# Moving everything after attention off GpSimd, one-instruction gate, and two parts of a product kept in TensorE's queue

## The chip, the core and the metric

The kernel runs on one core of a Trainium2 chip. A core has five engines that each work through their own instructions in order: TensorE (PE in the rows; its weight loads are PEld), VectorE (DVE), ScalarE (ACT), GpSimd (POOL) and SyncE (SP), which here issues nearly all DMAs. They wait for each other by semaphores. The metric is the time of one execution on the device, in microseconds (us).

## The reference

Rotary attention, then a mixture layer with a squared ReLU, then a second layer with a sigmoid gate. Only the two layers matter here, on 2304 tokens of 512 features, with 2048 features inside:

```python
h = x @ w_in;  r = np.maximum(h, 0.0);  x = (s * (r * r) + b) @ w_out       # first layer
h = x @ w_in2; g = h * (1.0 / (1.0 + np.exp(-1.702 * h)));  out = g @ w_out2  # second layer
```

Results are fp32, inputs of the products are split into a high and a low part, and three products of parts stand for one fp32 product.

## The kernel before

**Stages.** Attention runs first, with the first layer's early passes of 256 tokens woven in. When attention is over (`widen`, some 685 us into the run) its buffers are closed and `late` is set. Then come the end of the first layer (what is left of a pass of 256 tokens, pass 8, and pass 9 with 512) and, beside it, the preparation of the second layer's weights; then the second layer: passes 10 to 13 with 512 tokens and pass 14 with 256.

**Order.** TensorE's instructions are chained in the order in which the code is written (`mm` pins each to the one before); from `late` on VectorE's are too (`dv`). ScalarE's and GpSimd's are placed by a list scheduler. SyncE issues its DMAs in the scheduler's order, and each DMA that must wait holds all behind it.

**End of the first layer** (`first_layer`, L965). For each of 16 blocks of the inner features, TensorE makes 12 matmuls into a bank `l`, then 12 matmuls of the second product of the block two steps back (`SKEW = 2`). Between the two, each 256 columns pass ScalarE's Relu (L980), GpSimd's square (L990) and `s*r+b` (L991), ScalarE's copy to the high part (L992) and VectorE's low part (L993).

**Weights of the second layer.** Raw weights come by DMA into three buffers, `raw`; a buffer is filled again when its job is done (`fill`, `take`, `done_with`). `outer_make` (L820) takes two for each of 8 groups, turns fp64 words into fp32 (`to_f32`: L570 on ScalarE, L573, L578, L584 on VectorE), forms four differences on GpSimd (L844), and splits seven matrices into high (ScalarE, L834) and low (VectorE, L841). `combine` (L760) takes one raw per group: four sums on GpSimd (L790), highs L780, lows L787. `convert(budget)` draws such steps between blocks. The weights' scale and each pass's scale travel through DRAM (`share_top`: a DMA `tops<-xm`, then a broadcast DMA `xc<-tops`).

**Second layer** (`seven`, L1119). Each pass has 8 groups of 256 inner features. Both products of a group are done as seven half-size products (Strassen-Winograd). The first product's seven go alternately into two banks (`a0` and `b0`, tiles `l`): VectorE adds them into `cb` and `ca` (`add`, L1144; `u` is the first of them). The gate is ScalarE's Tanh into a tile `r` (L1148) and VectorE's `(r+1)*c` (L1152). Then come a difference on VectorE (L1190), three sums on GpSimd (`mixed`, L1155), and highs (ScalarE, L1158) and lows (VectorE, L1161) of seven operands: two in `gs`, four in `gb`, one in a spare weight slot `wo`. `rest`, `rest2` and `rest3` hold the last of it; `side(0)` to `side(2)` of the next group run them. The second product's first six parts (`products`) go to a `queue`; `between()` issues one at three places inside the next group's seven, and then the queue is emptied:

```python
                mixed = seven(n, g, x, between, side, need)
                yield
                tail.extend(mixed[3:6])
                while queue:
                    between()
                queue += second(n, g, mixed)
```

**Next tokens.** While a pass runs, `side` also loads and prepares the next pass's tokens (`sums_work`): maxima, scale, four differences (`sums_less`, on GpSimd, L1086), and seven splits (`x_high` L1067, `x_low` L1072).

Of the kernel before, what the change touches and what calls it, by code (L numbers as in the profile page):

```python
# [9 lines left out]
F32 = mybir.dt.float32  # L10
# [4 lines left out]
AF = mybir.ActivationFunctionType  # L15
# [8 lines left out]
X_TOP = 2.0**12  # L24
X_MIN = 2.0**-50
H_SCALE = 2.0**-23


@with_exitstack
def kernel(  # L30
# [729 lines left out]
    def combine(g, tag):  # L760
        pool = wpool if tag else late["m2"]
        raw = take()
        if tag == "stage":
            wc = [
                late["m2"].tile([128, k, 2, 256], F16, tag=tag, name=f"wc{g}{k}", bufs=3) for k in (4, 3)
            ]
            wc = [t[:, j] for t, k in zip(wc, (4, 3)) for j in range(k)]
        else:
            wc = pool.tile([128, 7, 2, 256], F16, tag=tag or f"wc{g}", name=f"wc{g}", bufs=1)
            wc = [wc[:, j] for j in range(7)]  # L770
        tmp = moe.tile([128, 2, 256], F32, tag="gg", name=f"sum{g}", bufs=3)
# [12 lines left out]

        def later():
            lo, src, col, hi = pend.pop(0)
            dv(nc.vector.scalar_tensor_tensor(lo, src, col, hi, op0=ALU.mult, op1=ALU.subtract))  # L787

        def mixed(o, x, y, op):
            nc.gpsimd.tensor_tensor(o, x, y, op=op)  # L790

        mixed(sa, a[:, 1, 0], a[:, 1, 1], ALU.add)
        halves(0, a[:, 0, 0], up)
        yield 0.1
        mixed(sb, sa, a[:, 0, 0], ALU.subtract)
# [24 lines left out]
    def outer_make(g, tag):  # L820
        up = wscale[:, 4:5]
        parts = [
            late["m2"].tile([128, k, 2, 256], F16, tag="g", name=f"wm{g}{k}", bufs=3) for k in (4, 3)
        ]
        tmp = moe.tile([128, 2, 256], F32, tag="gg", name=f"wsum{g}", bufs=3)

        pend = []

        def halves(j, src, n=1):
            o = parts[j // 4][:, j % 4 : j % 4 + n]  # L830
            hi, lo = o[:, :, 0], o[:, :, 1]
            if n == 1:
                hi, lo = hi[:, 0], lo[:, 0]
            pace(nc.scalar.activation(hi, src, AF.Copy, scale=up))  # L834
            pend.append((lo, src, hi))
            if len(pend) > 1:
                later()

        def later():
            lo, src, hi = pend.pop(0)  # L840
            dv(nc.vector.scalar_tensor_tensor(lo, src, up, hi, op0=ALU.mult, op1=ALU.subtract))  # L841

        def less(o, a, b):
            nc.gpsimd.tensor_tensor(o, a, b, op=ALU.subtract)  # L844
# [24 lines left out]
        done_with(1)  # L869
        nc.sync.dma_start(made[g][1], parts[1])  # L870
# [25 lines left out]
    late = {}  # L896
# [68 lines left out]
    def first_layer(n, f, w, xh, xl):  # L965
# [11 lines left out]
        for i in range(T // TB):  # L977
# [3 lines left out]
            if not late:  # L981
# [5 lines left out]
                    gl[:, cols], r, sb[:, 1:2], f32(gh[:, cols]), op0=ALU.add, op1=ALU.subtract  # L987
                )
                continue
            nc.gpsimd.tensor_tensor(r, r, r, op=ALU.mult)  # L990
            nc.gpsimd.tensor_scalar(r, r, sb[:, 0:1], sb[:, 1:2], op0=ALU.mult, op1=ALU.add)  # L991
            nc.scalar.copy(gh[:, cols], r)  # L992
            dv(nc.vector.tensor_tensor(gl[:, cols], r, f32(gh[:, cols]), op=ALU.subtract))  # L993
        return gh, gl
# [3 lines left out]
    def sums_load(n):  # L998
# [4 lines left out]
        x["m"] = late["m2"].tile([128, 9], F32, tag="xm", name=f"xm{n}", bufs=3)  # L1003
# [25 lines left out]
    def sums_scale(x):  # L1029
        m = x["m"]  # L1030
        scales(m[:, 5:6], m[:, 6:7], x["row"])
        for o, a, col, factor in ((7, 6, 2, 0.851), (8, 7, 5, 0.5 / 0.851)):
            if o == 7:
                factor = factor / H_SCALE
            dv(
                nc.vector.tensor_scalar(
                    m[:, o : o + 1], m[:, a : a + 1], wscale[:, col : col + 1], factor, op0=ALU.mult, op1=ALU.mult
                )
            )

# [40 lines left out]
                x_low(x, *x_high(x, j))  # L1081
                del x["todo"][j]

    def sums_less(x):
        for o, a, b in sums_parts(x):
            nc.gpsimd.tensor_tensor(o, a, b, op=ALU.subtract)  # L1086

    def sums_work(x):
        sums_top(x, 0, 0)
        yield  # L1090
        sums_top(x, 0, 1)
        sums_top(x, 1, 0)
        yield
        sums_top(x, 1, 1)
        yield
        yield
        sums_scale(x)
        pairs = [x_high(x, j) for j in (0, 3)]
# [20 lines left out]
    def seven(n, g, x, between, side, need):  # L1119
        T = PASSES[n][2]  # L1120
        half = T // 2
        nm = f"{n}_{g}"
        wc, xc, gain = combos[g], x["xc"], x["m"][:, 7:8]
        a0, b0 = (bank[:, 0:half] for bank in l1_banks[0:2])
        a1, b1 = a0, b0

# [16 lines left out]
        def add(o, ps, rest):  # L1143
            dv(nc.vector.scalar_tensor_tensor(o, ps, H_SCALE, rest, op0=ALU.mult, op1=ALU.add))  # L1144

        def curve(c, z):
            r = moe.tile([128, T], F32, tag="gg", name=f"r{nm}{z}", bufs=3)
            nc.scalar.activation(r, c, AF.Tanh, scale=gain)  # L1148
            return r

        def gate(c, r):
            dv(nc.vector.scalar_tensor_tensor(c, r, 1.0, c, op0=ALU.add, op1=ALU.mult))  # L1152

        def mixed(o, a, b, op):
# [40 lines left out]
        mixed(s3, a22, s3, ALU.subtract)
        mixed(a11, a11, s3, ALU.add)
        low(gb[:, 3, 1], a22, gb[:, 3, 0])
        high(gb[:, 0:2, 0], two(cb))

        def rest():  # L1200
            high(spare[:, 0, 0:half], a12)
            low(spare[:, 1, 0:half], a12, spare[:, 0, 0:half])
            mixed(a12, a12, s3, ALU.subtract)
            high(gb[:, 2, 0], a12)

        def rest2():
            low(gb[:, 0:2, 1], two(cb), gb[:, 0:2, 0])
# [19 lines left out]
    def products(n, g, made_g):  # L1227
# [105 lines left out]
    def experts():  # L1333
# [134 lines left out]
        for n in range(LAST0 + 1, len(PASSES)):  # L1468
            x = ahead.pop(n)
            for g in range(NG):  # L1470
                need(g, combos)

                def side(i):
                    if tail:
                        tail.pop(0)()
                    if n + 1 < len(PASSES):
                        x2nd = ahead.setdefault(n + 1, {})
                        if (g, i) == (0, 1):
                            x2nd.update(sums_load(n + 1))
# [12 lines left out]
                queue += second(n, g, mixed)  # L1492
                yield
# [264 lines left out]
```

## Time and profile before

| what | us |
|---|---|
| median of 3 runs (lowest, highest) | 1236.63 (1235.91, 1239.54) |
| the profiled execution itself | 1236.13 |
| its span, first to last instruction | 1234.3 |
| busy: PE, DVE, ACT, POOL | 1079.2, 959.7, 725.8, 478.6 |
| 0 to 686: attention and what is woven in | 686 |
| 686 to 868: end of the first layer, weights | 182 |
| 868 to 1234.3: second layer | 366.3 |

The profiled execution's own time is its span and 1.8 us around it. Times inside the profile count from the span's start. A matmul that follows others starts some 0.11 us after the one before but is listed with its whole duration, so a busy TensorE is not one at its peak.

### The profile page before, as it was taken

Reading aid. Unit: us, or ns where it says so; the run is one execution under the profiler, and the core shown is the slowest. Engines: PE = TensorE matmul, PEld = TensorE weight load, DVE = VectorE, ACT = ScalarE, POOL = GpSimd, SP = SyncE. Lnnn points to the kernel's source line nnn. Section 1 sums busy time; section 2 is a strip of 40 time slices with the busy share of each in tenths; the row PEclk is TensorE's granted clock in tenths of the full one; section 3 lists DMA queues with packets and bytes.
Section 4 is the critical chain, followed back from the end, with each engine's and each line's share of the span. In section 5 each row is a group of like instructions: output and inputs, shape, how many; then the busy total and the mean of one; then the engine's idle time right before and its main releaser. Section 6 shows DMA issues by size and latency. Waiting matters only on the chain.

```text
span 1234.3 us, 24890 instructions
## 1 busy us (share of the span) xinstructions
PE 1079.2 (87%) x8888; PEld 962.4 (78%) x8888; DVE 959.7 (78%) x2114; ACT 725.8 (59%) x1587; POOL 478.6 (39%) x557
## 2 busy tenths in 40 slices
PE   3676767898999999999999898878899898999997
PEld 2555557797888999999999786656788787888886
DVE  4877768999877887777776588756978887788876
ACT  2877766786665656576664564546554464554554
POOL 3344524344334332421111587866432424223222
PEclk9887988999999999999999899989999999999999
DMA  5776878899888889877776678754102001001010
GB/s 146 226 231 199 263 209 285 273 340 301 248 254 264 276 259 283 253 238 234 236 202 134 207 259 307 269 130 162 65 3 56 16 23 48 3 19 36 3 36 18
DMA packets 152778, 216.42 MB, mean 175 GB/s; under 512 B 34384, under 2 KB 107472, under 8 KB 152656
## 3 DMA queue, kind: packets, MB, share of 16 engines
q1 hardware_dynamic: 151792, 214.26, 55.9%
q8 instruction: 70, 1.15, 0.4%
q10 hardware_dynamic: 864, 0.59, 0.2%
q14 instruction: 52, 0.43, 0.1%
HBM read 157.65 MB, written 50.07 MB: 168 GB/s over the span
## 4 chain that ended last, share of the span: by engine, by line
PE 41%; DVE 23%; DMA 17%; ACT 7%; issue 5%; POOL 5%; SPq 2%; DVEq 0%; ACTq 0%; POOLq 0%
PE l L100 17%; PE acc L100 13%; PE t L100 3%; PE s L100 3%; DMA top<-in_moe_w_in_dram 3%; PE av L100 3%; DMA qb<-qsp 2%; DMA raw<-in_moe_w_out_dram 2%; DVE pt L499 2%; DVE P L432 2%; DMA w2f<-top 2%; DMA raw<-w2f 2%; POOL r L991 1%; DVE c L1152 1%; DVE wm L841 1%
## 5 line engine op out<-in xcount | busy, mean ns | idle before, releaser
L476 POOL TENSOR_SCALAR P<-P,st 128x576 f32<-128x576 f32 x108 | 85.0, 787 | 319.1 <-DVE st L475 185.8
L100 PE MATMUL l<-xc,wc 128*128 128x256 f16 (+1 forms) x1680 | 196.7, 264 | 10.5 <-DVE u L1144 6.7
L100 PEld LDWEIGHTS <-wc 128*128 128x128 f16 x1680 | 153.5, 98 | 32.4 <-issue 15.3
L100 PE MATMUL acc<-g,w 128*128 128x256 f32 (+1 forms) x1056 | 165.1, 304 | 14.5 <-DVE g L993 9.2
L100 PEld LDWEIGHTS acc<-g,w 128*128 128x128 f32 x1056 | 142.8, 194 | 25.7 <-DVE g L993 13.7
L442 ACT ACTIVATE P<-P,st 128x576 f32<-128x576 f32 x144 | 111.6, 775 | 65.3 <-DVE P L432 57.0
L1155 POOL TENSOR_TENSOR c<-c,c 128x256 f32<-128x256 f32 (+1 forms) x80 | 57.7, 721 | 236.3 <-DVE gs L1161 208.6
L432 DVE TENSOR_SCALAR_CACHE_REDUCE P<-s 128x576 f32<-128x576 f32 x144 | 108.0, 750 | 46.4 <-PE s L100 45.2
L100 PE MATMUL t<-ident,P 128*128 128x128 f32 x720 | 109.6, 286 | 29.1 <-DVE pt L499 18.7
L100 PE MATMUL l<-xh,w 128*128 128x256 f32 x616 | 126.7, 289 | 5.6 <-DVE r L982 2.9
L100 PEld LDWEIGHTS t<-ident,P 128*128 128x128 f32 x720 | 85.0, 147 | 38.4 <-issue 26.1
L100 PEld LDWEIGHTS l<-xh,w 128*128 128x128 f32 x616 | 101.9, 192 | 7.7 <-DVE r L982 3.7
L499 DVE TENSOR_TENSOR pt<-t,pt 128x640 f16<-128x640 f32 x108 | 88.3, 818 | 17.3 <-ACT pt L498 15.9
L1148 ACT ACTIVATE r<-c,xm 128x512 f32<-128x512 f32 (+1 forms) x80 | 54.3, 679 | 79.9 <-DVE c L1144 78.6
L100 PEld LDWEIGHTS <-gb 128*128 128x128 f16 x864 | 83.8, 98 | 10.5 <-ACT gb L1158 0.7
L100 PE MATMUL l<-xl,w 128*128 128x256 f32 x308 | 87.6, 284 | 1.2 <-DVE xl L948 1.2
L100 PE MATMUL s<-k,qb 128*128 128x320 f32 x480 | 87.0, 308 | 1.9 <-DVE pt L503 1.8
L100 PE MATMUL acc<-g,ws 128*128 128x256 f32 (+1 forms) x480 | 77.4, 309 | 11.0 <-ACT g L992 8.5
L275 POOL TENSOR_TENSOR rot<-nat,tab 128x288 f32<-128x288 f32 x60 | 52.9, 903 | 80.0 <-DMA nat<-in_k_dram 34.7
L498 ACT CAST pt<-t 128x640 f16<-128x640 f32 x108 | 73.8, 684 | 12.7 <-PE t L100 11.8
L100 PEld LDWEIGHTS s<-k,qb 128*128 128x128 f32 x480 | 72.4, 192 | 8.4 <-issue 3.1
L100 PEld LDWEIGHTS acc<-g,ws 128*128 128x128 f32 x480 | 65.3, 194 | 17.0 <-ACT g L992 9.8
(179 smaller groups left out, 2598.9 us busy)
## 6 DMA issues: line engine op xcount, KB each, us to landing
ws<-wd SPq DMA_DIRECT2D x80, 512.0 KB, 5.8
k<-ksp SPq DMA_DIRECT2D x24, 576.0 KB, 6.3
stage<-in_moe_w_in_dram SPq DMA_DIRECT2D x16, 512.0 KB, 5.5
stage<-in_moe_w_out_dram SPq DMA_DIRECT2D x16, 512.0 KB, 6.4
top<-in_moe_w_in_dram SPq DMA_DIRECT2D x32, 256.0 KB, 3.3
wo<-in_moe_w_out_dram SPq DMA_DIRECT2D x32, 256.0 KB, 5.6
raw<-in_moe_w_out_dram SPq DMA_DIRECT2D x16, 512.0 KB, 4.9
wd<-w SPq DMA_DIRECT2D x10, 512.0 KB, 4.0
```

The lines of the kernel that those rows point to most:

```text
L100: pin(nc.tensor.matmul(*args, **kw))
L275: eng.tensor_tensor(rot[:, :, e], st["nat"][:, :, 1 - e], tab[:, 2 - e], op=ALU.mult),
L432: ins = nc.vector.tensor_scalar(pr, ps[:, 192 : 192 + S], -Q_SCALE, None, op0=ALU.mult, op1=ALU.min, accum_out=st[:, 0:1],)
L442: nc.scalar.activation(pr, pr, AF.Exp, bias=st[:, 0:1], scale=-1.0, accum_out=total)
L476: pin(nc.gpsimd.tensor_scalar(pr, pr, st[:, 2:3], 1.0, op0=ALU.mult, op1=ALU.mult), "pool")
L498: nc.scalar.copy(hi, pc)
L499: nc.vector.tensor_tensor(lo, pc, hi, op=ALU.subtract)
L841: dv(nc.vector.scalar_tensor_tensor(lo, src, up, hi, op0=ALU.mult, op1=ALU.subtract))
L991: nc.gpsimd.tensor_scalar(r, r, sb[:, 0:1], sb[:, 1:2], op0=ALU.mult, op1=ALU.add)
L1148: nc.scalar.activation(r, c, AF.Tanh, scale=gain)
L1152: dv(nc.vector.scalar_tensor_tensor(c, r, 1.0, c, op0=ALU.add, op1=ALU.mult))
L1155: nc.gpsimd.tensor_tensor(o, a, b, op=op)
```

## The change

GpSimd's work from `late` on goes to other engines: squares and `s*r+b` to ScalarE (Square, Identity), the sums of `combine`, `outer_make`, `seven` and the next tokens to VectorE. The gate becomes one ScalarE instruction, Silu, in place; the scale that Tanh's form carried is now applied with the high and low parts (`lift`). The four differences of the next tokens are drawn one by one, and the first operands of a group are split per half. Two parts of the second product stay in the queue at the end of each group. Cut to its core:

```diff
@@ combine, outer_make, seven: mixed and less
-            nc.gpsimd.tensor_tensor(o, x, y, op=op)
+            dv(nc.vector.tensor_tensor(o, x, y, op=op))
@@ first_layer
-            nc.gpsimd.tensor_tensor(r, r, r, op=ALU.mult)
-            nc.gpsimd.tensor_scalar(r, r, sb[:, 0:1], sb[:, 1:2], op0=ALU.mult, op1=ALU.add)
+            nc.scalar.activation(r, r, AF.Square)
+            nc.scalar.activation(r, r, AF.Identity, bias=sb[:, 1:2], scale=sb[:, 0:1])
@@ sums_work
         sums_top(x, 1, 1)
-        yield
+        for o, a, b in sums_parts(x):
+            yield
+            mixed_x(o, a, b)
@@ seven
-        def curve(c, z):
-            r = moe.tile([128, T], F32, tag="gg", name=f"r{nm}{z}", bufs=3)
-            nc.scalar.activation(r, c, AF.Tanh, scale=gain)
-            return r
-        def gate(c, r):
-            dv(nc.vector.scalar_tensor_tensor(c, r, 1.0, c, op0=ALU.add, op1=ALU.mult))
+        def curve(c):
+            nc.scalar.activation(c, c, AF.Silu, scale=gain)
-            nc.scalar.copy(hi, c)
+            nc.scalar.activation(hi, c, AF.Copy, scale=lift)
-            dv(nc.vector.tensor_tensor(lo, c, hi, op=ALU.subtract))
+            dv(nc.vector.scalar_tensor_tensor(lo, c, lift, hi, op0=ALU.mult, op1=ALU.subtract))
@@ seven, behind the last product
-        rb, ra = curve(cb, 1), curve(ca, 0)
-        gate(cb, rb)
...
-        dv(nc.vector.tensor_tensor(s3, a11, s3, op=ALU.subtract))
-        high(gs[:, :, 0], two(cb))
-        gate(ca, ra)
-        low(gs[:, :, 1], two(cb), gs[:, :, 0])
+        curve(cb)
+        curve(ca)
+        s3 = p1
+        high(gs[:, 0, 0], a11)
+        mixed(s3, a11, a21, ALU.subtract)
+        low(gs[:, 0, 1], a11, gs[:, 0, 0])
+        high(gs[:, 1, 0], s3)
         high(gb[:, 3, 0], a22)
-        mixed(s3, a22, s3, ALU.subtract)
-        mixed(a11, a11, s3, ALU.add)
+        side(3)
+        mixed(a21, a21, a22, ALU.add)
+        low(gs[:, 1, 1], s3, gs[:, 1, 0])
+        mixed(a11, a21, a11, ALU.subtract)
         low(gb[:, 3, 1], a22, gb[:, 3, 0])
         high(gb[:, 0:2, 0], two(cb))
@@ experts
-                        if (g, i) == (3, 1):
-                            sums_less(x2nd)
-                        if i in (2, 3) and (g in (1, 2) or g > 3):
+                        if g and (i > 1 or i and g > 5):
                             next(x2nd["work"], None)
-                while queue:
+                while len(queue) > 2:
                     between()
```

**GpSimd's rows in the first layer's last pass, before.** `r_80` and `r_81` are the two halves of block 8, `sum_10403` and `sum_10672` temporaries of two `combine` jobs, `raw_10400` the raw weights of the second of them.

```order
L990 TENSOR_TENSOR r_80_10437<-r_80_10437 128x256
L790 TENSOR_TENSOR sum_10403<-raw_10274 128x256
L990 TENSOR_TENSOR r_81_10443<-r_81_10443 128x256
L790 TENSOR_TENSOR sum_10672<-raw_10400 128x256
L991 TENSOR_SCALAR r_80_10437<-r_80_10437,sb 128x256
L790 TENSOR_TENSOR sum_10403<-raw_10274,sum_10403 128x256
L991 TENSOR_SCALAR r_81_10443<-r_81_10443,sb 128x256
```

The change has no such rows on GpSimd. The same first sum of `raw_10400` stands on VectorE there, behind the low parts of block 12 (`g_12`) and the last splits of pass 10's tokens (`xc`):

```order
L994 TENSOR_TENSOR g_12_10644<-r_120_10645,g_12_10644 128x256
L994 TENSOR_TENSOR g_12_10644<-r_121_10651,g_12_10644 128x256
L1077 SCALAR_TENSOR_TENSOR xc_10147<-xt_1_10514,xm_10146,xc_10147 128x512
L1077 SCALAR_TENSOR_TENSOR xc_10147<-xr_1_10145,xm_10146,xc_10147 128x512
L791 TENSOR_TENSOR sum_10674<-raw_10400 128x256
L791 TENSOR_TENSOR sum_10674<-sum_10674,raw_10400 128x256
```

The sum that needs `raw_10400` moved from the middle of block 8 to behind block 12.

**TensorE's rows at the change of a group, before.** In the second layer's pass 10, `l_1774` and `l_9163` are the banks `a0` and `b0`, `wc_10341` and `wc_10402` the first product's weights of groups 2 and 3, `gs_2` and `gb_1` operands of the second product of groups 2 and 1, `acc` and `l_9165` its banks. Six matmuls with their weight loads make one part; one row of each part is shown.

```order
L100 MATMUL acc_3_10955<-wo_10150,gb_1_10961 128x256
...
L100 MATMUL l_9164<-wo_10150,gb_1_10961 128x256
...
L100 MATMUL l_9165<-wo_10150,gb_1_10961 128x256
...
L100 MATMUL l_1774<-xc_10147,wc_10402 128x256
...
L100 MATMUL l_9163<-xc_10147,wc_10402 128x256
...
L100 MATMUL acc_0_10952<-wo_10266,gs_2_11077 128x256
```

The same place in the change:

```order
L101 MATMUL acc_1_10939<-wo_10150,gs_1_10946 128x256
...
L101 MATMUL acc_2_10940<-wo_10150,gb_1_10947 128x256
...
L101 MATMUL acc_3_10941<-wo_10150,gb_1_10947 128x256
...
L101 MATMUL l_1774<-xc_10147,wc_10402 128x256
...
L101 MATMUL l_9163<-xc_10147,wc_10402 128x256
...
L101 MATMUL l_9164<-wo_10150,gb_1_10947 128x256
...
L101 MATMUL l_9165<-wo_10150,gb_1_10947 128x256
...
L101 MATMUL acc_0_10938<-wo_10266,gs_2_11062 128x256
```

Where three of the old group's parts stood last and the new group's first part of the second product came after two products, now two old parts stand among the new products, and the part that reads `gs` of the group before comes behind six of the seven.

**VectorE's rows at the end of a group, before** (group 5 of pass 11, which prepares pass 12's tokens; `c_51` and `c_50` are `cb` and `ca`):

```order
L1144 SCALAR_TENSOR_TENSOR c_50_12436<-l_1774,u_5_12438 128x256
L1152 SCALAR_TENSOR_TENSOR c_51_12435<-r_51_12516,c_51_12435 128x512
L1190 TENSOR_TENSOR c_51_12435<-c_51_12435 128x256
L1152 SCALAR_TENSOR_TENSOR c_50_12436<-r_50_12518,c_50_12436 128x512
L1161 TENSOR_TENSOR gs_5_12439<-c_51_12435,gs_5_12439 128x2x256
L1161 TENSOR_TENSOR gb_5_12440<-c_50_12436,gb_5_12440 128x256
L1072 SCALAR_TENSOR_TENSOR xc_11830<-xr_1_11828,xm_11829,xc_11830 128x512
L1144 SCALAR_TENSOR_TENSOR u_6_12553<-l_9163,p_6_12552 128x256
L1161 TENSOR_TENSOR wo_10767<-c_50_12436,wo_10767 128x256
```

And in the change, from the same add on:

```order
L1152 SCALAR_TENSOR_TENSOR c_50_12390<-l_1774,u_5_12392 128x256
L1158 TENSOR_TENSOR p_5_12391<-c_51_12389 128x256
L1164 SCALAR_TENSOR_TENSOR gs_5_12393<-c_51_12389,xm_10865,gs_5_12393 128x256
L1077 SCALAR_TENSOR_TENSOR xc_11803<-xr_0_11800,xm_11802,xc_11803 128x512
L1158 TENSOR_TENSOR c_51_12389<-c_51_12389,c_50_12390 128x256
L1164 SCALAR_TENSOR_TENSOR gs_5_12393<-p_5_12391,xm_10865,gs_5_12393 128x256
L1158 TENSOR_TENSOR c_51_12389<-c_51_12389 128x256
L1164 SCALAR_TENSOR_TENSOR gb_5_12394<-c_50_12390,xm_10865,gb_5_12394 128x256
L1152 SCALAR_TENSOR_TENSOR u_6_12515<-l_9163,p_6_12514 128x256
L1164 SCALAR_TENSOR_TENSOR gb_5_12394<-c_51_12389,xm_10865,gb_5_12394 128x2x256
```

The two gate rows (L1152 before) and the wide low part are gone, three sums have come from GpSimd, and the token split (`xc`) that stood directly ahead of the next group's `u` now stands ahead of the sums.

## Rows read from the trace of the kernel before

**Rows 1.** The page's parts 1 and 4: busy engines; the chain that ended last.

```profile
PE 1079.2 (87%) x8888; PEld 962.4 (78%) x8888; DVE 959.7 (78%) x2114; ACT 725.8 (59%) x1587; POOL 478.6 (39%) x557
...
PE 41%; DVE 23%; DMA 17%; ACT 7%; issue 5%; POOL 5%; SPq 2%; DVEq 0%; ACTq 0%; POOLq 0%
```

**Rows 2.** Windows: length, PE, PEld, DVE, ACT, POOL busy, granted clock, DMA share, GB/s.

```profile
686.00:868.00 182.00, 154.27 (x829) 127.75 (x828) 136.93 (x227) 99.27 (x228) 135.40 (x160) 0.95 0.67 224
868.00:1234.30 366.30, 340.78 (x3164) 296.17 (x3162) 296.13 (x632) 186.78 (x404) 110.70 (x138) 0.99 0.11 27
820.40:827.20 6.80, 4.20 (x9) 3.02 (x10) 1.88 (x4) 2.55 (x7) 5.54 (x10) 0.50 0.23 78
948.00:1028.00 80.00, 74.85 (x674) 65.42 (x672) 66.17 (x131) 40.42 (x82) 24.93 (x28) 1.00 0.11 28
1045.60:1052.50 6.90, 5.78 (x29) 3.94 (x28) 3.90 (x8) 1.41 (x3) 2.64 (x4) 0.51 0.00 0
```

**Rows 3.** TensorE's waits, 868 to 1234.3: total us, times, longest.

```profile
PE acc L100 <- DVE gs L1161: 8.7, 19, 2.4
PE l L100 <- DVE u L1144: 6.7, 14, 1.7
PE acc L100 <- ACT gs L1158: 3.5, 7, 1.4
```

**Rows 4.** Timeline around 962: start, duration, engine, line; [idle before].

```profile
960.41 1.07 DVE L1152 SCALAR_TENSOR_TENSOR c<-r,c 128x512 f32<-128x512 f32 x1
...
960.88 1.71 POOL L1086 TENSOR_TENSOR xt<-xr,xt 128x512 f32<-128x512 f32 x1
...
962.80 1.75 DVE L1152 SCALAR_TENSOR_TENSOR c<-r,c 128x512 f32<-128x512 f32 x1
...
963.64 0.28 PE L100 MATMUL acc<-wo,gs 128*128 128x256 f16 x1 [1.41 <-ACT gs L1158]
...
965.21 0.72 PE L100 MATMUL acc<-wo,gs 128*128 128x256 f16 x5 [1.29 <-DVE gs L1161]
```

**Rows 5.** Timeline around 913: VectorE and TensorE.

```profile
912.67 1.22 DVE L1072 SCALAR_TENSOR_TENSOR xc<-xr,xm,xc 128x512 f16<-128x512 f32 x1
...
914.28 0.81 PE L100 MATMUL l<-xc,wc 128*128 128x256 f16 x6 [0.42 <-DVE u L1144]
```

**Rows 6.** Costs by line, 868 to 1234.3: count | busy us, mean ns.

```profile
L1152 DVE SCALAR_TENSOR_TENSOR c<-r,c 128x512 f32<-128x512 f32 x64 | 46.8, 730 | 0.2
L1148 ACT ACTIVATE r<-c,xm 128x512 f32<-128x512 f32 x63 | 45.4, 721 | 72.7 <-DVE c L1144 71.4 <-DVE gb L1161 1.3
...
L1161 DVE TENSOR_TENSOR gb<-c,gb 128x256 f16<-128x256 f32 x72 | 33.8, 469 | 1.6 <-ACT gb L1158 0.9
```

**Rows 7.** ScalarE's table load: ns of one, shortest, median, longest.

```profile
L309 ACT ACT_TABLE_LOAD  x1: 1283/1283/1283, 0.7 to 0.7; - x1
```

**Rows 8.** TensorE's waits, 686 to 868.

```profile
PE acc L100 <- ACT g L992: 12.7, 8, 5.8
PE acc L100 <- DVE g L993: 11.7, 12, 2.6
```

**Rows 9.** Timeline, 813 to 823.

```profile
813.55 8.41 SPq L745 DMA_DIRECT2D raw<-w2f  x2
...
819.61 0.72 POOL L790 TENSOR_TENSOR sum<-raw 128x256 f32<-128x256 f32 x1 [5.47 <-DMA raw<-w2f]
...
820.90 0.40 ACT L992 CAST g<-r 128x256 fp32r<-128x256 f32 x1 [6.97 <-POOL r L991]
...
822.59 0.79 PE L100 MATMUL acc<-g,ws 128*128 128x512 f32 x1 [5.78 <-ACT g L992]
```

**Rows 10.** Costs by line, 686 to 868.

```profile
L991 POOL TENSOR_SCALAR r<-r,sb 128x256 f32<-128x256 f32 x49 | 45.0, 921 | 1.9
...
L990 POOL TENSOR_TENSOR r<-r 128x256 f32<-128x256 f32 x49 | 37.3, 770 | 31.0 <-ACT r L980 30.6
...
L992 ACT CAST g<-r 128x256 fp32r<-128x256 f32 x49 | 19.2, 401 | 27.1 <-POOL r L991 26.5
```

More of the change, by code (lines that the diff above doesn't have):

```diff
@@ L26 @@
 H_SCALE = 2.0**-23
+G_TOP = 2.0**-22
 @with_exitstack
@@ L843, in less @@
         def less(o, a, b):
-            nc.gpsimd.tensor_tensor(o, a, b, op=ALU.subtract)
+            dv(nc.vector.tensor_tensor(o, a, b, op=ALU.subtract))
         one, _ = yield from to_f32(take())
@@ L1002, in sums_load @@
         x["raw"] = [f32(x_tile(f"xr{n}_{i}"))[:, 0 : 2 * T] for i in range(2)]
-        x["m"] = late["m2"].tile([128, 9], F32, tag="xm", name=f"xm{n}", bufs=3)
+        x["m"] = late["m2"].tile([128, 10], F32, tag="xm", name=f"xm{n}", bufs=3)
         finals[n] = x["m"][:, 8:9]
@@ L1031, in sums_scale @@
         scales(m[:, 5:6], m[:, 6:7], x["row"])
-        for o, a, col, factor in ((7, 6, 2, 0.851), (8, 7, 5, 0.5 / 0.851)):
-            if o == 7:
-                factor = factor / H_SCALE
+        for o, a, col, factor in (
+            (7, 6, 2, 1.702 / H_SCALE),
+            (9, 5, 0, G_TOP / 1.702),
+            (8, 6, 2, 1.0 / G_TOP),
+            (8, 8, 5, 1.0),
+        ):
+            b = m[:, a : a + 1]
             dv(
                 nc.vector.tensor_scalar(
-                    m[:, o : o + 1], m[:, a : a + 1], wscale[:, col : col + 1], factor, op0=ALU.mult, op1=ALU.mult
+                    m[:, o : o + 1], b, wscale[:, col : col + 1], factor, op0=ALU.mult, op1=ALU.mult
                 )
@@ L1082, in sums_split, with mixed_x @@
                 del x["todo"][j]
-    def sums_less(x):
-        for o, a, b in sums_parts(x):
-            nc.gpsimd.tensor_tensor(o, a, b, op=ALU.subtract)
+    def mixed_x(o, a, b):
+        dv(nc.vector.tensor_tensor(o, a, b, op=ALU.subtract))
     def sums_work(x):
@@ L1094, in sums_work @@
         sums_top(x, 1, 1)
-        yield
+        for o, a, b in sums_parts(x):
+            yield
+            mixed_x(o, a, b)
         yield
@@ L1123, in seven @@
         wc, xc, gain = combos[g], x["xc"], x["m"][:, 7:8]
+        lift = x["m"][:, 9:10]
         a0, b0 = (bank[:, 0:half] for bank in l1_banks[0:2])
@@ L1144, in add @@
             dv(nc.vector.scalar_tensor_tensor(o, ps, H_SCALE, rest, op0=ALU.mult, op1=ALU.add))
-        def curve(c, z):
-            r = moe.tile([128, T], F32, tag="gg", name=f"r{nm}{z}", bufs=3)
-            nc.scalar.activation(r, c, AF.Tanh, scale=gain)
-            return r
-        def gate(c, r):
-            dv(nc.vector.scalar_tensor_tensor(c, r, 1.0, c, op0=ALU.add, op1=ALU.mult))
+        def curve(c):
+            nc.scalar.activation(c, c, AF.Silu, scale=gain)
         def mixed(o, a, b, op):
-            nc.gpsimd.tensor_tensor(o, a, b, op=op)
+            dv(nc.vector.tensor_tensor(o, a, b, op=op))
         def high(hi, c):
-            nc.scalar.copy(hi, c)
+            nc.scalar.activation(hi, c, AF.Copy, scale=lift)
         def low(lo, c, hi):
-            dv(nc.vector.tensor_tensor(lo, c, hi, op=ALU.subtract))
+            dv(nc.vector.scalar_tensor_tensor(lo, c, lift, hi, op0=ALU.mult, op1=ALU.subtract))
         def two(t):
@@ L1185, in seven @@
         add(ca[:, half:T], a1, u2)
-        rb, ra = curve(cb, 1), curve(ca, 0)
-        gate(cb, rb)
-        a11, s3 = cb[:, 0:half], cb[:, half:T]
+        curve(cb)
+        curve(ca)
+        a11, a21 = cb[:, 0:half], cb[:, half:T]
         a12, a22 = ca[:, 0:half], ca[:, half:T]
-        dv(nc.vector.tensor_tensor(s3, a11, s3, op=ALU.subtract))
-        high(gs[:, :, 0], two(cb))
-        gate(ca, ra)
-        low(gs[:, :, 1], two(cb), gs[:, :, 0])
+        s3 = p1
[3 more added lines that the diff above has]
+        high(gs[:, 1, 0], s3)
         high(gb[:, 3, 0], a22)
-        mixed(s3, a22, s3, ALU.subtract)
-        mixed(a11, a11, s3, ALU.add)
+        side(3)
+        mixed(a21, a21, a22, ALU.add)
+        low(gs[:, 1, 1], s3, gs[:, 1, 0])
+        mixed(a11, a21, a11, ALU.subtract)
         low(gb[:, 3, 1], a22, gb[:, 3, 0])
@@ L1201, in rest, with rest2 @@
             high(spare[:, 0, 0:half], a12)
+            low(gb[:, 0:2, 1], two(cb), gb[:, 0:2, 0])
+            mixed(a22, a12, a11, ALU.subtract)
+            high(gb[:, 2, 0], a22)
+        def rest2():
             low(spare[:, 1, 0:half], a12, spare[:, 0, 0:half])
[L1203 to L1207, printed above, removed]
         def rest3():
-            low(gb[:, 2, 1], a12, gb[:, 2, 0])
-        side(3)
+            low(gb[:, 2, 1], a22, gb[:, 2, 0])
         return gs, gb, spare, rest, rest2, rest3
@@ L1231, in products @@
         w = outer[g]
-        left = (gs[:, 0], gs[:, 1], gb[:, 3], gb[:, 1], gb[:, 0], gb[:, 2], spare)
+        left = (gs[:, 0], gs[:, 1], gb[:, 3], gb[:, 0], gb[:, 1], gb[:, 2], spare)
         right = (w[0], w[4], w[6], w[5], w[1], w[3], w[2])
```

## Prediction, made before the changed kernel was run

> **What bounds the kernel now.** I read the page first. TensorE is busy 87% of the span, and in the chain that ended last it holds only 41%, with VectorE 23%, DMA 17%, ScalarE and GpSimd 12% [rows 1]. The reader is to see that TensorE carries the kernel and that what can be won is the time in which others keep it waiting. Up to 686 us both programs have the same order on every engine, so that part is taken as unchanged, and I asked for windows of the rest [rows 2]: 182 us for the end of the first layer, where GpSimd is busy 135.4 us, VectorE 136.9 and the granted clock averages 0.95, and 366.3 us for the second layer, where GpSimd is busy 110.7, VectorE 296.1 and the clock averages 0.99. Then TensorE's waits in each.
>
> In the second layer three rows make 18.9 us in 40 waits [rows 3]: 12.2 for the parts `gs`, 6.7 for `u`. A wait costs more than its listed idle. In [rows 4] one matmul takes 0.28, five take 0.72, so they follow each other by (0.72 - 0.28) / 4 = 0.11; after a wait the first one's whole 0.28 is exposed, 0.17 more each time. The waits then cost 18.9 + 40 x 0.17 = 25.7. And the clock was granted at half, the 1.2 GHz level, from 1045.6 to 1052.5, after a wait of 2.4: 6.9 x 0.49 = 3.4.
>
> At the end of the first layer TensorE waits 24.4 us in 20 times for `g` [rows 8], with 20 x 0.17 = 3.4 on top. The longest, 5.78, has a clear cause [rows 9]: a transfer into `raw` was issued at 813.55 and took 8.41; GpSimd stood 5.47 at the head of its queue for it, with the finished half of block 8 behind it; ScalarE waited 6.97 for that half and TensorE 5.78 for ScalarE. The clock fell to half here as well (820.4 to 827.2), while TensorE stood still. Over the stage a clock of 0.95 is 0.05 x 182 = 9.
>
> So some 29 us can be recovered in the second layer and 24.4 + 3.4 + 9 = 37 in the first; 66 in all.
>
> **The change, second layer (cost against the profiled execution, 1236.13).**
>
> *Two parts stay queued.* In TensorE's order, seven parts of six matmuls stand now between the product that releases a group's first curve and the first part that reads `gs`, and thirteen in the change: 7 x 0.66 = 4.6 us of cover become 13 x 0.66 = 8.6. What has to fit: two curves, a high, a difference, a high and a low, about 0.72 + 0.72 + 0.4 + 0.47 + 0.4 + 0.47 = 3.2 when nothing interferes (durations of such rows in [rows 6, 10]), and up to 4.6 + 2.4 = 7.0 as late as the longest wait shows it now. Both lie under 8.6. The `gs` waits, 12.2 + 26 x 0.17 = 16.6, should go, save those of the last group, which has no group behind it (1.1): **-15.5**. If the cover did nothing, the shorter chain alone would still take the 1.5 us stretches of the next point, so the lower bound is half, -8.
>
> *GpSimd's rows go to VectorE, and the gate goes.* While GpSimd runs, VectorE's rows with two inputs in SBUF grow: the gate takes 0.730 on average, but 1.07 and 1.75 beside GpSimd's difference of 1.71 [rows 4, 6]. TensorE then waits 1.41 and 1.29. Per group VectorE loses two gates, 2 x 0.730 = 1.46, and gets three sums, at 0.469 (a low part of the same size) 1.41: even, and without the stretches. In a pass it is busy 66.2 of 80 us, 8.3 per group, against TensorE's 84 matmuls x 0.11 = 9.2. There is room, but little.
>
> *The `u` waits* (6.7 + 14 x 0.17 = 9.1): a long token row stands ahead of `u`, such as the 1.22 at 912.67, and TensorE waits 0.42 [rows 5]. In the change the token row stands ahead of the sums and is shorter without GpSimd, but six token pieces now come from VectorE and pass 10 starts with weights work still running. Between none and all I take half: **-4.5**.
>
> *The clock*: without the long wait before it, its 3.4 should not occur: **-3.4**; bound 0.
>
> *New costs.* ScalarE's order has one more table load, before the first Silu; the row at the start took 1283 ns [rows 7]: +1.3. The Trainium skill ("ScalarE: Activation LUTs", *What ACT_TABLE_LOAD costs*) counts a drain of about 1.38 us with it, 2.66 in all; by that the sum would be 1.4 us later. Silu itself has no row; I take Tanh's 721 ns for the same 512 columns, between a plain copy of two times 256 (0.80) and that. The `lift` pointer in highs and lows, narrower first operands (one more row on each engine per group) and the small pieces in the late groups of three passes: 0.15 x 32 = 4.8 if all of it shows, 0 if hidden by the longer cover; I take **+6** with the table load, since pass 14's half-size groups have less cover.
>
> Second layer: -15.5 - 4.5 - 3.4 + 6 = **-17**; bounds -8 and -29.
>
> **End of the first layer.** *The blocked queue.* The same sum now waits on VectorE four blocks later (the order rows show it behind block 12), so the transfer should have landed: -(5.78 + 0.17), and the half clock from 822.59 to 827.2, 4.6 x 0.5 = 2.3: **-8**. If `raw` came that late again, the wait would sit ahead of all of VectorE; bound 0.
>
> *The shorter relay.* A half passes Relu, square, `s*r+b`, copy and low. GpSimd's two rows take 0.770 + 0.921 [rows 10]; on ScalarE, at the copy's 0.401 each, 0.80: 0.9 us shorter, and with no other engine between. The other 19 waits are 24.4 - 5.78 = 18.6, on average 0.98, so 0.9 is nearly all of each; with their 3.2 and the rest of the clock (9 - 2.3 = 6.7) 28.5 can be had. Against it: ScalarE gets 98 rows at 0.4, 39 us on its 99.3, and VectorE 62 of GpSimd's 160 rows, 29 us on its 136.9. Between 0 and all I take a little under half: **-12**.
>
> First layer: **-20**; bounds +5 (a fuller ScalarE) and -35.
>
> **Sum.** 1236.1 - 17 - 20 = **1199**. The profiled execution stands 0.5 below the median of 1236.63, which is inside the runs' own spread, so I predict 1199 for the median.
>
> **The rivals.**
>
> *A. The end of the first layer gains nothing.* VectorE's rows there would be 136.9 + 29 = 166 us, if they don't become shorter, in a stage that I want to bring down to 162; all in one pinned order, with the weights' splits, the lows of blocks and the new sums behind each other. ScalarE comes to 138. For it: VectorE has no room without the stretches. Against it: those rows are stretched now. With the blocked queue gone (-8) and five lost to the fuller queues: 1236 - 17 - 3 = **1216**. The Trainium skill ("ScalarE: Activation LUTs", *Rules for kernel authors*) says of relu, add and mul to use VectorE, not ScalarE; by that, squares on ScalarE would be slow and this rival likelier. The trace does not bear it out here: ScalarE's 401 ns for 256 fp32 columns [rows 10] is no longer than VectorE's 469 [rows 6].
>
> *B. Nearly all waits go.* The cover of 8.6 is twice the chain, the relay is shorter than the mean wait, and both half clocks vanish: 85% of 66 is 56: **1180**. Against it: VectorE is busy for 8.3 of 9.2 us per group.
>
> *C. VectorE and ScalarE wait for each other (slower).* Each group now alternates between them seven times on the way to `gs` and `gb`, in pinned order. VectorE idles (80 - 66.2) / 8 = 1.7 us per group today; if it idles as long, a pass stays at 80 us, and the second layer gains nothing. From 1.7 + 20 / 32 = 2.3 us of idle per group it eats the first layer's gain; at 2.6 the second layer is 32 x 0.9 = 29 longer, and the time 1236 - 20 + 29 = **1245**. Against it: the parts' cover has grown by 4 us, and a row that waits 0.1 more does not reach TensorE.
>
> *D. VectorE's rows are not shorter without GpSimd.* Then the sums are pure addition, 1.4 us per group in a stage with 0.9 to spare, and only the queue, the clock and the blocked transfer are won: about **1228**.
>
> **How the numbers follow.** The forecast's own case (1188 to 1210) 0.55, A 0.2, B 0.15, C 0.04, D 0.04, nothing 0.02. Runs differ by about 0.3%, 3.7 us, which is also what a measurement can tell from no change: faster means below 1233. Faster 0.55 + 0.2 + 0.15 + 0.03 = 0.93, same 0.03, slower 0.04. The range reaches from just under B, 1177, to a little beyond A, 1221; above lie C, D and the worse half of the bounds.
>
> **What would show it.** GpSimd has no rows past 686. TensorE's waits for `gs` are gone but for the last group; its wait of 5.8 near 820 and both stretches at half clock are gone. A pass of the second layer falls from 80 to about 75.5 us; VectorE's low parts of 256 columns take some 0.42 with no tail above 0.7. The end of the first layer takes about 162 us, with ScalarE busy near 138 and VectorE below 150. I am wrong if VectorE's busy time there stays near 166, or if TensorE's waits now name VectorE's sums or ScalarE's highs, or if the table load or a `raw` transfer appears in front of a long wait.

## The result, and the profile after

The changed kernel takes 1194.18 us (median of 4 runs, 1191.39 to 1197.18) against 1237.22 of the kernel before in the same comparison; the ratio is 0.9651, 95% interval 0.9623 to 0.9678. Predicted were 1199, range 1177 to 1221. The profiled execution has a span of 1192.1.

The page's parts 1 and 4 of the changed kernel, beside [rows 1]:

```profile
PE 1060.6 (89%) x8888; PEld 958.6 (80%) x8888; DVE 940.0 (79%) x2284; ACT 785.5 (66%) x1726; POOL 232.9 (20%) x259
...
PE 56%; DVE 16%; DMA 12%; ACT 9%; issue 4%; SPq 1%; POOL 0%; DVEq 0%; ACTq 0%; POOLq 0%
```

TensorE's share of the last chain rose from 41% to 56%, and GpSimd is out of it. I cut both traces where the first matmul of pass 10 starts, at 858.1 before and 840.0 now; before it, near 686, the same matmul starts within 0.5 us in both. So the end of the first layer is some 18 us shorter and the rest of the span 24. Windows of the changed kernel: the two stages, and pass 11.

```profile
685.40:840.00 154.60, 137.58 (x777) 118.30 (x777) 118.71 (x269) 127.40 (x308) 0.00 (x0) 0.99 0.80 263
840.00:1192.10 352.10, 339.49 (x3217) 301.49 (x3216) 296.43 (x758) 218.16 (x464) 0.00 (x0) 1.00 0.11 29
915.01:989.08 74.07, 73.56 (x674) 65.74 (x672) 63.72 (x153) 45.01 (x90) 0.00 (x0) 1.00 0.12 30
```

GpSimd has no rows there. In pass 11 VectorE, with GpSimd's sums added, is busy 63.7 us in a pass of 74.1, where it was 66.2 of 80 [rows 2]. TensorE's waits past 840, and at the end of the first layer (685.4 to 840), beside [rows 3, 8]:

```profile
PE l L101 <- DVE u L1152: 2.7, 4, 1.2
PE l L101 <- ACT p L1170: 2.5, 6, 1.0
PE l L101 <- DVE c L1152: 1.8, 1, 1.8
PE acc L101 <- ACT gb L1161: 0.3, 1, 0.3
PE acc L101 <- DVE gb L1164: 0.2, 1, 0.2
```

```profile
PE acc L101 <- DVE g L994: 15.0, 13, 1.9
PE acc L101 <- DMA ws<-wd: 1.1, 1, 1.1
PE l L101 <- ACT r L981: 1.0, 2, 0.6
```

No wait for `gs` is left, not even in the last group, and the wait of 5.78 at block 8 has no successor. At the end of the first layer 15 of the 24.4 us for `g` remain, in 13 shorter pieces. In front of six of them, 7.2 us in all, VectorE stood for a transfer of raw weights; the rows below are its waits there in all, and the worst of the six places:

```profile
DVE raw L574 <- DMA raw<-in_moe_w_out_dram: 15.1, 6, 3.7
```

```profile
755.39 0.43 DVE L574 TENSOR_SCALAR raw<-raw 128x512 uint32<-128x512 uint32 x1 [3.74 <-DMA raw<-in_moe_w_out_dram]
755.74 0.75 DVE L994 TENSOR_TENSOR g<-r,g 128x256 fp32r<-128x256 f32 x2
```

VectorE stands 3.74 us for raw weights, and the block's low parts (L994), whose highs ended at 753.7, run right behind it. TensorE starts at 756.54, 1.81 late. In front of six more of the 13, another 7.0 us, VectorE waited for nothing: the low parts stood behind the weights' splits and, since the change, their sums in the one order of VectorE. The worst of these:

```profile
800.49 0.87 DVE L788 SCALAR_TENSOR_TENSOR wc<-sum,wscale,wc 128x256 f16<-128x256 f32 x2
...
801.28 0.75 DVE L994 TENSOR_TENSOR g<-r,g 128x256 fp32r<-128x256 f32 x2
...
802.09 2.79 PE L101 MATMUL acc<-g,w 128*128 128x512 f32 x11 [1.83 <-DVE g L994]
```

The highs of this block had ended at 797.5. Costs by line at the end of the first layer, two rows of the kernel before (686 to 868) and then the changed kernel: VectorE's rows of 256 columns are at their short length, 477 and 480 ns for the low parts of weights that took 796 and 642.

```profile
L841 DVE SCALAR_TENSOR_TENSOR wm<-raw,wscale,wm 128x256 f16<-128x256 f32 x16 | 12.7, 796 | 4.4 <-ACT wm L834 4.4
...
L787 DVE SCALAR_TENSOR_TENSOR wc<-sum,wscale,wc 128x256 f16<-128x256 f32 x28 | 18.0, 642 | 11.7 <-ACT wc L780 11.6
```

```profile
L992 ACT ACTIVATE r<-r,sb 128x256 f32<-128x256 f32 x47 | 26.7, 595 | 0.3
...
L994 DVE TENSOR_TENSOR g<-r,g 128x256 fp32r<-128x256 f32 x47 | 18.5, 419 | 7.8 <-ACT g L993 7.8
...
L788 DVE SCALAR_TENSOR_TENSOR wc<-sum,wscale,wc 128x256 f16<-128x256 f32 x24 | 11.3, 480 | 2.2 <-ACT wc L781 2.1
...
L842 DVE SCALAR_TENSOR_TENSOR wm<-raw,wscale,wm 128x256 f16<-128x256 f32 x16 | 7.6, 477 | 0.1
```

### The profile page after: what moved, and what is told of

It reads as the page before. It is cut to its first block, busy times and chain, and to the rows that moved or that the text cites. A ratio compares the mean times of both kernels' runs of the same rounds, so it can differ in the third digit from the quotient of the medians.

```text
span 1192.1 us, 24697 instructions
## 1 busy us (share of the span) xinstructions
PE 1060.6 (89%) x8888; PEld 958.6 (80%) x8888; DVE 940.0 (79%) x2284; ACT 785.5 (66%) x1726; POOL 232.9 (20%) x259
## 4 chain that ended last, share of the span: by engine, by line
PE 56%; DVE 16%; DMA 12%; ACT 9%; issue 4%; SPq 1%; POOL 0%; DVEq 0%; ACTq 0%; POOLq 0%
PE l L101 24%; PE acc L101 17%; PE s L101 5%; PE t L101 4%; PE av L101 4%; DMA raw<-in_moe_w_out_dram 3%; DVE pt L500 2%; DVE P L433 2%; DMA qb<-qsp 2%; PE r L104 1%; DMA wo<-in_moe_w_out_dram 1%; DVE wc L788 1%; ACT P L443 1%; DMA top<-in_moe_w_in_dram 1%; DMA stage<-in_moe_w_in_dram 1%
## 5 line engine op out<-in xcount | busy, mean ns | idle before, releaser
L101 PE MATMUL l<-xc,wc 128*128 128x256 f16 (+1 forms) x1680 | 192.8, 262 | 7.5 <-DVE u L1152 2.7
L101 PE MATMUL acc<-g,w 128*128 128x256 f32 (+1 forms) x1056 | 162.7, 302 | 14.0 <-DVE g L994 13.1
L101 PEld LDWEIGHTS acc<-g,w 128*128 128x128 f32 x1056 | 141.5, 191 | 22.7 <-DVE g L994 16.3
L1155 ACT ACTIVATE c<-c,xm 128x512 f32<-128x512 f32 (+1 forms) x80 | 54.1, 676 | 66.6 <-DVE c L1152 65.3
L499 ACT CAST pt<-t 128x640 f16<-128x640 f32 x108 | 73.9, 684 | 12.9 <-PE t L101 12.7
L981 ACT ACTIVATE r<-l 128x256 f32<-128x256 f32 x144 | 53.3, 377 | 41.0 <-PE l L101 35.5
L101 PE MATMUL acc<-g,ws 128*128 128x256 f32 (+1 forms) x480 | 73.3, 300 | 2.9 <-DVE g L994 1.8
L1161 ACT ACTIVATE gb<-c,xm 128x256 f16<-128x256 f32 (+2 forms) x120 | 65.0, 542 | 9.1 <-DVE c L1158 8.5
L986 ACT ACTIVATE g<-r,sb 128x256 fp32r<-128x256 f32 x95 | 48.5, 510 | 33.8 <-DVE r L983 33.4
```

The costliest lines, as they stand in the source:

```text
L101: pin(nc.tensor.matmul(*args, **kw))
L499: nc.scalar.copy(hi, pc)
L981: nc.scalar.activation(r, ps[:, cols], AF.Relu)
L986: nc.scalar.activation(gh[:, cols], r, AF.Identity, bias=sb[:, 1:2])
L1155: nc.scalar.activation(c, c, AF.Silu, scale=gain)
L1161: nc.scalar.activation(hi, c, AF.Copy, scale=lift)
```

## The experiments

The total came out near the forecast, but a total says nothing of its terms, so each part was undone in the changed kernel or made alone in the kernel before. Later comparisons ran where the kernel before takes 1241 to 1243, so ratios are compared; 0.001 is 1.24 us, and the changed kernel stands at 0.9651. A ratio is uncertain by 3 to 5 us. The table therefore has two lengths from each run's profile as well: the end of the first layer, from the program's 4900th matmul (the same one in all kernels, at 685.1 to 693.2) to pass 10's first product, and the second layer from there on. They come from one execution each; where kernels share the code of a stage, its length differs by up to 4 us at the end of the first layer and by about 1 in the second (save one, the later conversion).

| kernel | ratio | first layer's end, us | second layer, us |
|---|---|---|---|
| before | 1 | 172.1 | 376.2 |
| changed | 0.9651 | 154.4 | 352.2 |
| changed, queue emptied | 0.9631 | 153.1 | 351.5 |
| changed, second layer's sums on GpSimd | 0.9651 | 151.8 | 355.6 |
| changed, both of these | 0.9667 | 152.8 | 355.3 |
| changed, tokens as before | 0.9691 | 152.2 | 360.9 |
| changed, Tanh and gate | 0.9810 | 153.9 | 375.4 |
| before, Silu | 0.9893 | 175.8 | 364.3 |
| before, two parts queued | 0.9964 | 175.5 | 369.5 |
| changed, relay on GpSimd | 0.9699 | 161.7 | 353.4 |
| changed, weights' sums on GpSimd | 0.9742 | 163.8 | 353.5 |
| before, relay on ScalarE | 0.9911 | 164.0 | 376.4 |
| changed, later conversion | 0.9715 | 158.5 | 357.1 |
| the same, larger steps | 0.9682 | 157.6 | 352.5 |

**The queue emptied again.**

```diff
-                while len(queue) > 2:
+                while queue:
```

> The changed kernel with the queue emptied at the end of each group, as before. Theory of the prediction (the cover of 8.6 us instead of 4.6 is what removes the gs waits): the second layer gets 8 to 15 us longer, so about 1202 to 1209 us, with TensorE's waits for gs back in 20 or more groups. Rival (the chain itself became short: in the changed kernel's steady group the gs low parts end 2.5 and 3.8 us after the last add that releases the first curve, less than the 4.6 us of the old order): within 3 us of 1194, with gs waits under 3 us in all.

Ratio 0.9631 (0.9606 to 0.9655): no slower than the changed kernel. TensorE's waits from pass 10 on:

```profile
PE l L101 <- ACT p L1170: 2.4, 5, 1.0
PE l L101 <- DVE c L1152: 1.8, 1, 1.8
PE l L101 <- DVE u L1152: 1.5, 3, 0.5
PE acc L101 <- DVE gb L1164: 0.2, 1, 0.2
```

There is not one wait for `gs`, with the old cover of 4.6 us. The rival holds: in the changed kernel the longer cover is not what removes them.

**The second layer's sums on GpSimd again, alone and with the queue emptied.**

```diff
@@ seven
         def mixed(o, a, b, op):
-            dv(nc.vector.tensor_tensor(o, a, b, op=op))
+            nc.gpsimd.tensor_tensor(o, a, b, op=op)
```

> The changed kernel with the three sums of each group of the second layer back on GpSimd (the next tokens' differences stay on VectorE). If the longer cover hides their length: 1194 to 1198 us, although VectorE's rows with two inputs in SBUF stretch again beside GpSimd (means up from 0.42 to about 0.5, single rows above 0.8). If VectorE's short rows are what pays: 1202 to 1210, with waits for u and gs back.

> Both of the last two edits: sums of the second layer on GpSimd and the queue emptied at each group. If each edit alone is nearly free because the other covers for it, the two together cost far more than their sum: 1208 to 1215 us. If the costs are independent, their sum within 3 us.

Ratios 0.9651 (0.9623 to 0.968) and 0.9667 (0.9639 to 0.9694): by the middle nothing and 2 us, both inside the noise. The profiles put it at some 3 us of second layer, with the queue emptied or not. VectorE's rows do stretch (the 256-column `gb` lows from 477 to 644 ns in the second kernel), but TensorE hardly feels it; of waits for `gs` there is one, of 0.2. So the two are no equal cures that cover for each other.

**The tokens prepared as before**, four differences in one lump on GpSimd.

```diff
-    def mixed_x(o, a, b):
-        dv(nc.vector.tensor_tensor(o, a, b, op=ALU.subtract))
+    def sums_less(x):
+        for o, a, b in sums_parts(x):
+            nc.gpsimd.tensor_tensor(o, a, b, op=ALU.subtract)
...
@@ experts
-                        if g and (i > 1 or i and g > 5):
+                        if (g, i) == (3, 1):
+                            sums_less(x2nd)
+                        if i in (2, 3) and (g in (1, 2) or g > 3):
```

> The changed kernel with the next tokens prepared as before: their four differences in one lump on GpSimd in group 3, steps drawn at the old places. In the kernel before, the time from one group to the next is 8.5 us in quiet groups, but 12.2, 15.2 and 9.6 at the lump in passes 11 to 13 and 10.2 three groups later. If the lump is the main cause of the second layer's loss and the two queued parts and Silu don't cover it: 6 to 14 us slower than the changed kernel, in the same groups. If the gate (two VectorE rows and a second crossing between engines) was the cause, the lump meets short chains and costs 0 to 3 us.

Ratio 0.9691 (0.9658 to 0.9724), by the middle 5 us slower, with overlapping intervals; the second layer is 9 longer. By the starts of the groups' first products in the timeline, the lump's groups take 9.6, 12.7 and 8.5 us in passes 11 to 13, where the changed kernel has 8.5 and the kernel before 12.2, 15.2 and 9.6. The lump costs something, in its own place, and less than in the kernel before; by the ratio that is between the two outcomes expected, by the profile the first.

**Tanh and its gate again**, the lift's scale set to 1.

```diff
@@ seven, behind the last product
-        curve(cb)
-        curve(ca)
+        rb = curve(cb, 1)
+        gate(cb, rb)
+        ra = curve(ca, 0)
...
+        gate(ca, ra)
```

> The changed kernel with the gate as before: Tanh on ScalarE, (r+1)*c on VectorE, the scale of the lift set to 1. VectorE gets 2 x 0.69 us per group more, 8.0 + 1.4 = 9.4 busy per group against 8.5 to 9.2 of TensorE. If the gate is a main cause: 8 to 15 us slower than the changed kernel, spread over all groups. If the lump of the tokens was: within 4 us.

Ratio 0.981 (0.9772 to 0.9847): 20 us slower, the largest single part. With it goes all that the second layer had gained: 375.4 us, where the kernel before has 376.2. Pass 11 in windows, and the first of TensorE's waits:

```profile
921.80:1000.60 78.80, 74.57 (x674) 65.65 (x673) 72.89 (x169) 44.64 (x90) 0.00 (x0) 1.00 0.11 29
```

```profile
PE l L101 <- DVE u L1152: 20.5, 32, 2.1
```

VectorE is busy 72.9 of 78.8 us and waits in that pass for 4.8 us in all, never more than 0.5 at a time; TensorE waits for `u` 32 times, and a quiet group (one that neither begins the pass nor splits tokens) takes 9.1 us in place of 8.5. VectorE is the bound. A kernel with the gate and the sums on different engines, and the rest as in the change, was not run.

**Silu alone in the kernel before**, and **two parts in the queue alone in the kernel before** (each edit as in the diff of the change).

> The kernel before with Silu as its gate and the lift, all else as it was. If the gate is a main cause: 10 to 18 us faster than before (ratio 0.985 to 0.992). If the lump on GpSimd is: 1 to 6 us faster (0.995 to 0.999), the groups at the lump still long.

> The kernel before with two parts kept in the queue, all else as it was. The longest gs wait there makes the operands 7.0 us late, under the new cover of 8.6. If cover is an equal cure for the gs waits while GpSimd's lump is still there: 10 to 16 us faster than before (ratio 0.987 to 0.992). If the lateness only moves on to u, which waits behind the same VectorE rows: 0 to 4 us (0.997 to 1.0).

Ratios 0.9893 (0.986 to 0.9926) and 0.9964 (0.9939 to 0.9988): 13 us and 4.5 us faster; the second layer is 12 and 7 shorter. With Silu the lump's groups fall from 12.2, 15.2 and 9.6 to 10.6, 10.1 and 8.6, which is 7.7 of the 12: among the rows that the lump stretched were the gates (1.07 and 1.75 in [rows 4]). TensorE's waits for `gs` and `u` from 868 on, first with two parts queued, then with Silu:

```profile
PE l L100 <- DVE u L1144: 15.2, 21, 2.5
...
PE acc L100 <- DVE gs L1161: 0.2, 1, 0.2
```

```profile
PE l L101 <- DVE u L1149: 5.8, 8, 1.5
PE acc L101 <- DVE gs L1161: 3.2, 8, 0.5
```

The longer cover does abolish the `gs` waits (8.7 and 3.5 in [rows 3]), and the `u` waits grow from 6.7 to 15.2: `u` is an add in the same VectorE order, behind the rows that were late. Most of the wait moved on by one product. With Silu alone the `gs` waits fall from 12.2 to 3.6 us under the old cover.

**The relay on GpSimd again; the weights' sums on GpSimd again; the relay alone moved in the kernel before.**

```diff
-            nc.scalar.activation(r, r, AF.Square)
-            nc.scalar.activation(r, r, AF.Identity, bias=sb[:, 1:2], scale=sb[:, 0:1])
+            nc.gpsimd.tensor_tensor(r, r, r, op=ALU.mult)
+            nc.gpsimd.tensor_scalar(r, r, sb[:, 0:1], sb[:, 1:2], op0=ALU.mult, op1=ALU.add)
```

```diff
@@ combine: mixed; outer_make: less, likewise
         def mixed(o, x, y, op):
-            dv(nc.vector.tensor_tensor(o, x, y, op=op))
+            nc.gpsimd.tensor_tensor(o, x, y, op=op)
```

> The changed kernel with square and s*r+b of the first layer's end back on GpSimd. Theory of the prediction (a relay 0.9 us longer per half, and GpSimd stretching VectorE): the stage between 685 and 840 gets 8 to 14 us longer, about 1202 to 1208 us. Rival (what is left there is VectorE standing for transfers into raw, 23 us of idle in the changed kernel, and the relay hides behind it): 1194 to 1197.

> The changed kernel with the sums of the second layer's weights (combine and outer_make) back on GpSimd, the first layer's relay left on ScalarE. If moving them to VectorE was needed for the gain: pass 10 begins 4 to 10 us later than the 838 to 843 us of the runs so far, about 1202 to 1208 us on the first chip. If VectorE has room and the rows cost the same on either engine: within 3 us of the changed kernel.

> The kernel before with square and s*r+b on ScalarE, all else as it was: GpSimd keeps the sums only. Theory of the prediction (the blocked queue 8 us and the shorter relay 12): pass 10 begins 15 to 20 us earlier than in the kernel before, ratio about 0.985 to 0.988. Rival (only the block goes, since GpSimd's sums still stretch VectorE): 5 to 9 us, ratio 0.993 to 0.996.

Ratios 0.9699 (0.9675 to 0.9722), 0.9742 (0.9719 to 0.9764) and 0.9911 (0.9885 to 0.9937). So the relay is worth 6 us in the changed kernel, the move of the sums 11, and the relay alone 11 in the kernel before; for the relay both times that is between the two outcomes expected. By the table the first layer's end is 161.7 and 163.8 where the kernels with the changed code have 151.8 to 154.4 (six profiles), and 164.0 where those with the code of before have 172.1 to 175.8 (three): 7 to 10, 9 to 12 and 8 to 12 us. The timeline with the weights' sums on GpSimd says why the relay alone is not enough:

```profile
820.65 1.40 POOL L791 TENSOR_TENSOR sum<-raw 128x256 f32<-128x256 f32 x2 [10.05 <-DMA raw<-w2f]
...
822.09 0.51 ACT L781 ACTIVATE wc<-sum,wscale 128x256 f16<-128x256 f32 x1 [6.82 <-POOL sum L791]
...
823.25 0.79 PE L101 MATMUL acc<-g,ws 128*128 128x512 f32 x1 [5.35 <-ACT g L993]
```

It is the stall of [rows 9] with one engine exchanged: the transfer holds GpSimd's sum, the sum holds ScalarE's high of it, and behind that high stands the block's copy. The relay alone in the kernel before has it too, with 5.87 on ScalarE. It is gone where the sums are on VectorE and stand later, with the relay on either engine: with the relay alone back on GpSimd no wait of TensorE's there is longer than 2.3. With the weights' sums on GpSimd VectorE's rows stretch too (the low parts of `g` from 419 to 535 ns), so the 11 us are the stall and the stretching together.

**A later conversion**, to take VectorE off the transfers, and the same with larger steps per block.

```diff
+        yield 2.0
         two, _ = yield from to_f32(take())
@@ second kernel only
-                convert(3.5 if T == 512 else 2.2)
+                convert(4.5 if T == 512 else 2.8)
```

> The changed kernel with one added step of delay (2.0 of the planner's units, some 3 us) ahead of the second conversion in outer_make, the row at which VectorE stands for a transfer into raw (six times, 15 us of its idle, while finished blocks' low parts wait behind it). If these head-of-queue waits are what is left of TensorE's 15 us for g: those waits fall under 6 us and the kernel gets 4 to 9 us faster than the changed one. If the transfers only set the pace of the weights: the waits move, and later weights delay pass 10's first groups, 0 to 6 us slower.

> The same delay with larger steps per block (2.8 and 4.5 units in place of 2.2 and 3.5), so that the weights are not later. If the standing for transfers is the cause: 5 to 10 us faster than the changed kernel. If bigger bunches of weight work ahead of a block delay its low parts as much: within 3 us.

Ratios 0.9715 (0.9676 to 0.9755) and 0.9682 (0.9662 to 0.9702): slower by 8 and 4 by the middle, so the hope of 4 to 10 us did not come true in either. VectorE's standing at L574 fell from 15.1 to 6.3 and 3.4 us, as intended, but in the first kernel ScalarE stood instead:

```profile
803.86 0.52 ACT L835 ACTIVATE wm<-raw,wscale 128x256 f16<-128x256 f32 x1 [8.70 <-DMA wod<-wm]
```

A buffer of split weights was not yet written out, and pass 10's first group then took 16.3 us, where it takes 11.9. In the second TensorE's waits for `g` sank only to 11.6, and the first layer's end took 157.6 us. Taking VectorE off these transfers does not help here. What would is not settled; a fourth buffer for `raw` was not tried.

## Why the prediction held, and where its steps did not

**GpSimd gone and VectorE's rows short:** as forecast. Both half-clock stretches of [rows 2] are gone too; the mean granted clock is 0.99 and 1.00 in the two stages, where it was 0.95 and 0.99. A pass takes 74.1 us. Of the signs of being wrong one showed in part: a transfer into `raw` stands in front of six of TensorE's waits, 0.8 to 1.8 us each.

**First layer, -20; measured -18.** The terms were mis-sized against each other. The relay was put at 12 and is worth 6 by the ratio, 7 to 10 by the stage. Its rows are longer than the prediction took them: Square takes 413 ns and `s*r+b`, with scale and bias from a tile, 595, not twice the 401 of a copy, so that the relay is 0.7 us shorter and not 0.9. And the waits were not the relay's alone: the blocks' low parts stand in VectorE's one order behind transfers, sums and splits. How much each held back was not separated. The blocked queue was rightly tied to the sum's later place; but the move of the sums was priced at 8, for that one stall and the half clock behind it, and is worth 11. Rival A's 166 us of VectorE work did not come about: VectorE is busy 118.7 us in the stage, because the stretched rows became short. What A said of the order shows on a smaller scale, in the 7.0 us behind sums and splits.

**Second layer, -17; measured -24, and by another route.** The step that failed is the first, "two parts stay queued ... -15.5". Undoing it costs nothing, and alone it brings 4.5 us by the ratio, since the lateness mostly passes to `u`. What took those waits is near what the prediction wrote down as the lower bound, a shorter chain; but the chain is short for want of the gates, not of stretched rows. With the sums back on GpSimd and the queue emptied the rows are stretched, and the waits stay away. The edit that the prediction costed "even" carries most of the gain: VectorE's busy time in the second layer did stay nearly even (296.4 us, where it was 303.2), yet without Silu the other edits bring nothing there (375.4 against 376.2), since with the gates and the sums both on VectorE a pass needs 72.9 us of its time and TensorE waits in most groups. Silu alone, in the kernel before, brings 12; the tokens' differences, undone alone, cost 9, and the sums 3. Together that is the measured 24, though the first was measured from the other end.

The room was read too wide as well. The prediction set VectorE's mean of 8.3 us per group against 9.2 for 84 matmuls. A pass gives its first group more than the others; a quiet one has 78 matmuls and takes 8.5 us, and VectorE is busy 7.2 of them in the changed kernel and 8.4 of 9.1 with the gate.

**The new costs, +6,** hardly appeared: pass 14's groups take 4.6 where they took 4.8, and in passes 10 to 12 only one of the later groups takes 9.2 and not 8.5, the one in which VectorE computes the next tokens' scale (ten small rows, 894.9 to 896.8 in pass 10) and splits a token row ahead of `u`. Silu takes 720 ns for 512 columns, as Tanh did. The `u` waits kept 2.7 of 6.7, a little better than half.

**The table load** is one row between a high part and the first Silu:

```profile
847.38 0.49 ACT L781 ACTIVATE wc<-raw,wscale 128x256 f16<-128x256 f32 x1
847.89 1.28 ACT L1155 ACT_TABLE_LOAD   x1
849.19 0.72 ACT L1155 ACTIVATE c<-c,xm 128x512 f32<-128x512 f32 x1
```

The row before it ended at 847.87, so it cost some 1.3 us in all. The 2.66 that the Trainium skill ("ScalarE: Activation LUTs", *What ACT_TABLE_LOAD costs*) counts for a switch do not show here.

So the time was near the forecast by luck: two errors in opposite directions stood in the second layer (cover too high, gate at zero) and two in the first (relay too high, sums too low). The forecast's 5 us of error is their remainder.

## What to carry to other kernels

More work queued ahead of a wait only helps if the late engine has nothing else that is needed soon; look which row stands behind the late one in the same order before crediting the cover. An edit that leaves an engine's busy time even can still be the largest, if it is what makes room for another edit or if the rows it removes are those that a neighbour stretches: undo each part alone, a right total does not confirm the terms. And a stall at the head of a queue was cured here by placing the waiting row later, not by changing the engine of those it blocks.

## What was not expected of the hardware

ScalarE's rows show a price for operands read from a tile: at the end of the first layer 256 columns take 400 ns as a plain copy (L993), 413 as Square (L991), about 500 with a scale from a tile (L781) and 595 with scale and bias (L992). A scale given as a number adds nothing: 376 (L1170) beside Relu's 381 (L981), both reading a bank. In the second layer the same highs took 405 as plain copies before, and 498 with `lift`:

```profile
L1158 ACT CAST gb<-c 128x256 f16<-128x256 f32 x72 | 29.1, 405 | 13.6 <-POOL c L1155 11.0 <-DVE c L1152 2.0
...
L1161 ACT ACTIVATE gb<-c,xm 128x256 f16<-128x256 f32 x72 | 35.9, 498 | 3.9 <-DVE c L1158 3.4
```
